# A Hedgehog attention with an S4 convolution on one core: second products of ten far rows as extra moving columns, near tables for two quarters, output weights last

## The chip, the core and the metric

The kernel runs on one core of a Trainium2 chip. The metric is the device time of the launch in microseconds (us). The profile is one execution recorded by the hardware profiler; its engines are PE (TensorE: PE for the matmuls, PEld for the weight loads that overlap them), DVE (VectorE), ACT (ScalarE), POOL (GpSimd) and SP (SyncE, which issues nearly all DMAs here).

## The reference

Two independent branches whose outputs stand side by side in one array of 2048 x 896 in bf16. The first is linear attention with learned softmax features, 16 heads of 28 features:

```python
qkv = x @ wqkv                                   # x: 1 x 2048 x 448
pq = einsum("bhsd,hdf->bhsf", q, w_phi); pk = einsum("bhsd,hdf->bhsf", k, w_phi)
phi_q = concat([softmax(pq), softmax(-pq)]); phi_k = concat([softmax(pk), softmax(-pk)])
kv = einsum("bhsf,bhsd->bhfd", phi_k, v); z = phi_k.sum(over s)
o = einsum(phi_q, kv) / (einsum(phi_q, z) + 1e-6)
a = o @ wo
```

The second is a state-space convolution over 448 channels with 256 complex states each:

```python
l = arange(2048).astype(bf16)                    # rounded: 641 different positions are left
P = exp(dt * A * l);  K = einsum("dn,dnl,dn->dl", C, P, dt * B).real
y = irfft(rfft(pad(u)) * rfft(pad(K)), 4096)[:2048]   # length 4096, per channel
b = y + u * Dskip
```

## The kernel before

**How the order is set.** The kernel does not issue instructions as its Python functions run. Each helper appends a pair (engine, function) to a list, 1008 of them, and `prog.run(ORDER)` at the end issues them in the order of a written-out list of numbers. Three more lists belong to it: `PLACES` gives the SBUF address of each buffer, `SLOTS` the PSUM banks of each group of matmuls, and `PICKS` says for each of 200 copies and scalings whether ScalarE (A) or VectorE (V) does it. Every engine works through its own part of the order in sequence. Since the helpers issue everything, the profile's lines are theirs: L177 `tt` (VectorE, two tensors), L194 `recip` (VectorE reciprocal), L198 `af` (ScalarE, any function), L205 `copy`, L208 `scaled`, L211 `square`, L215 `mset` (POOL), L220 `mms` (matmuls), L230 `transposes`, L236 and L240 the DMAs. So one reads the profile by shape.

**The convolution.** The 448 channels are worked in four quarters (`qt`) of 112; a quarter has QC = 224 columns (a state half for each channel) on 128 partitions, and NCOL = 896 columns are all four. A position is written as one of 16 high parts plus one of 40 low parts (`HI`, `LO`), so that exp(dt A l) is a product. For one quarter, `tables` makes

- the near low rows: `args` lets TensorE multiply the angles and dampings (AT, TH, each held as a bf16 part and a bf16 rest) by scaled identities of PID into PSUM, `rotations` takes sine and cosine, `dampings` exp of plus and minus multiples, and `damp` multiplies these into rows 2 to 15 of W;
- the far low rows: `far` makes rows 16 to 39. `step` adds 256 to the positions of some rows by a complex product with PW[256], which is two products, one subtraction and one addition on VectorE; `squares` doubles the positions of four rows;
- the high rows U_, in `hi_tables`, by doubling;
- the kernel K at all positions: `build_k` contracts the states on TensorE. One accumulation runs on 32 of the array's columns, so four groups (g) work side by side, and 80 columns move (40 low rows by two channels). A copy moves the sums to TS, and `scatter_k` sends them through DRAM to the layout that the transform reads (KT).

`kernel_spectrum` transforms KT (matmuls of 112 columns against the table F), `signal_spectrum` does the same to u, in two halves, after adding and subtracting u and its reversal; the reversed odd rows are made by TensorE with a reversal matrix (REV), and the result waits in DRAM (SUd). `conv` multiplies the spectra on VectorE (`prod`), combines the products either on VectorE (`finish`) or, for the blocks in `ON_PE`, on TensorE (`finish_pe`), and transforms back in `inverse`, 36 matmuls of 112 columns for each block, of which four add u times Dskip.

**The attention.** `fold_weights` multiplies the query and key weights by w_phi. `key_side` runs over eight pairs of row tiles: matmuls for K and V, exponentials of both signs, a transposing DMA (ET), the softmax sums on TensorE, their reciprocals on VectorE, and the state sums kv, which gather in PSUM over all eight pairs (matmuls of 116 columns, L220, whose moving operand VR holds 4 of every 16 values). At the end it multiplies the states by the output weights once, M = KV @ wo, with eight transposes and eight matmuls. `query_side` takes four blocks of 512 rows: query matmuls, exponentials, denominators and reciprocals, a trip through DRAM (SCd) that spreads the softmax weights over partitions (SB), the product EQ = EQ x SB, and 32 matmuls of 448 columns with M.

**The order around the change.** The program calls, in this order, `tables(0)`, `key_side`, `tables(1)`, then query blocks, spectra, convolutions and the other two `tables`; `ORDER` interleaves them far more finely. On SP's queue stand the loads of parameters, of u (four loads of 0.46 MB), of the table G1, of weights and the transposing loads of x.

## Time and profile before

| what | value |
|---|---|
| device time, three runs | 235.61, 237.11 and 239.20 us; median 237.11 us |
| span of the profiled execution | 233.5 us (the record gives no separate time of that execution; the median is 3.6 us above its span) |
| busy PE / DVE / ACT | 208.1 / 216.8 / 183.9 us |
| instructions | 7103, of them 3044 on PE |
| DMA | 36.40 MB, 156 GB/s on average |
| chain that ended last | PE 51%, ACT 17%, DVE 13%, DMA 5% of the span |

A busy time sums the durations of an engine's instructions. Matmuls are pipelined, so a matmul's duration holds latency that overlaps the next one; the distance from one start to the next is the better price. In a row such as "L220 PE MATMUL psum<-sbuf 128\*32 128x80 bf16 x896 | 18.3, 258 | 0.0" stand the line, the engine, the operation, where it writes and reads, the shape (for matmuls the stationary tile and the moving operand), the count, the busy time of all, the mean duration of one in ns, and the idle time before them. A row of a stretch gives from and to, and then the busy times of PE, PEld, DVE, ACT and POOL with the instructions in brackets, the clock granted to TensorE (1.00 is full), the busy share of the DMA engines and what they moved in GB/s. A row of the chain gives the start, the length, the engine and the line.

### The profile page before, as it was taken

The numbers are of one execution on the slowest core, as the hardware profiler recorded it, in microseconds if no ns is written. First come the engines' busy times: TensorE is split into PE (matmuls) and PEld (weight loads), VectorE is DVE, ScalarE is ACT, GpSimd is POOL, SyncE is SP. The second block draws the span as 40 slices with busy tenths as digits, with TensorE's granted clock in tenths as the row PEclk, the third lists the DMA queues.
The fourth block names the chain that finished last, engine by engine and source line by source line (L and its number), as shares of the span: only waits on it lengthen the run. The fifth ranks groups of instructions, "written<-read, shape, count | busy, mean of one in ns | idle before, by whom it ended". The sixth has DMA issues, their size and how long they took to land.

```text
span 233.5 us, 7103 instructions
## 1 busy us (share of the span) xinstructions
PE 208.1 (89%) x3044; PEld 152.8 (65%) x3044; DVE 216.8 (93%) x267; ACT 183.9 (79%) x321; POOL 4.6 (2%) x20
## 2 busy tenths in 40 slices
PE   1173899998999999999987999999999999999994
PEld 1161446564557655589765678885579968689993
DVE  1799999999999999989999979999999999999980
ACT  3999999999999999999998998698328451355331
POOL 4000000000000100000000000000000000000000
PEclk9999999999999999999999999999999999999999
DMA  5999910499239999826865899872696890489643
GB/s 154 237 218 272 151 37 1 167 150 235 71 59 190 147 176 257 152 71 155 206 156 144 99 255 225 226 114 61 70 368 131 199 277 10 63 185 242 121 100 81
DMA packets 81640, 36.40 MB, mean 156 GB/s; under 512 B 65480, under 2 KB 79688, under 8 KB 81224
## 3 DMA queue, kind: packets, MB, share of 16 engines
q1 hardware_dynamic: 81368, 35.71, 73.3%
q8 instruction: 24, 0.39, 0.7%
q10 hardware_dynamic: 240, 0.23, 0.3%
q14 instruction: 8, 0.07, 0.1%
HBM read 19.44 MB, written 8.62 MB: 120 GB/s over the span
## 4 chain that ended last, share of the span: by engine, by line
PE 51%; ACT 17%; DVE 13%; DMA 5%; issue 3%; SPq 0%; ACTq 0%
PE psum L220 51%; DVE sbuf L177 11%; ACT sbuf L198 8%; ACT sbuf L205 7%; DMA sbuf<-sbuf 3%; DMA sbuf<-KTd 2%; ACT L198 1%; DVE sbuf L205 1%; DVE sbuf L194 0%; ACT sbuf L211 0%; SPq L240 0%; DVE sbuf L212 0%; ACT sbuf L208 0%; DVE sbuf L208 0%; PE psum L230 0%
## 5 line engine op out<-in xcount | busy, mean ns | idle before, releaser
L220 PE MATMUL psum<-sbuf 128*128 128x112 bf16 (+9 forms) x3000 | 206.2, 252 | 21.4 <-ACT sbuf L205 7.8
L177 DVE TENSOR_TENSOR sbuf<-sbuf 128x896 bf16<-128x896 bf16 (+11 forms) x222 | 197.3, 956 | 7.2 <-ACT sbuf L198 4.3
L220 PEld LDWEIGHTS <-sbuf 128*128 128x128 bf16 (+3 forms) x3000 | 150.1, 114 | 75.3 <-issue 18.2
L205 ACT CAST sbuf<-psum 128x448 bf16<-128x448 f32 (+4 forms) x129 | 79.7, 672 | 38.0 <-PE psum L220 37.3
L198 ACT ACTIVATE sbuf<-psum 128x448 bf16<-128x448 f32 (+4 forms) x110 | 65.5, 721 | 0.5 <-PE psum L220 0.4
L211 ACT ACTIVATE sbuf<-sbuf 128x896 bf16<-128x896 bf16 x14 | 14.2, 1024 | 4.0 <-DVE sbuf L177 4.0
L198 ACT ACTIVATE sbuf<-psum,sbuf 128x896 f32<-128x896 f32 (+3 forms) x17 | 13.6, 835 | 0.0
L208 ACT ACTIVATE sbuf<-sbuf 128x896 bf16<-128x896 bf16 (+2 forms) x10 | 10.9, 1091 | 1.4 <-DVE sbuf L299 0.8
L198 ACT ACT_TABLE_LOAD x8 | 10.3, 1283 | 1.4 <-PEq L900 1.3
L205 ACT COPY sbuf<-sbuf 128x224 bf16<-128x224 bf16 (+2 forms) x18 | 8.9, 512 | 0.0
L205 DVE CAST sbuf<-psum 128x448 bf16<-128x448 f32 (+3 forms) x8 | 5.3, 690 | 2.3 <-PE psum L220 1.7
L215 POOL MEMSET sbuf<- 128x224 bf16 (+4 forms) x15 | 4.2, 314 | 153.3 <-PE psum L220 153.1
L205 ACT COPY sbuf<-psum 112x896 bf16<-112x896 bf16 (+2 forms) x13 | 6.8, 549 | 0.1
L177 DVE TENSOR_TENSOR sbuf<-psum,sbuf 128x448 bf16<-128x448 f32 (+3 forms) x12 | 5.1, 444 | 0.1
L194 DVE RECIPROCAL sbuf<-psum 128x64 bf16<-128x64 f32 x8 | 4.3, 546 | 0.4 <-ACT sbuf L198 0.3
L230 PEld LDWEIGHTS <-sbuf 112*112 112x112 bf16 (+1 forms) x44 | 3.1, 128 | 1.8 <-DVE sbuf L177 0.8
L230 PE MATMUL psum<-sbuf 112*112 112x112 bf16 (+1 forms) x44 | 3.6, 215 | 0.6 <-DVE sbuf L177 0.6
L212 DVE TENSOR_TENSOR sbuf<-sbuf 128x896 bf16<-128x896 bf16 (+1 forms) x3 | 3.3, 1087 | 0.0
L194 DVE RECIPROCAL sbuf<-sbuf 128x64 f32<-128x64 f32 x4 | 2.2, 545 | 0.0
L189 DVE SCALAR_TENSOR_TENSOR sbuf<-sbuf 128x64 f32<-128x64 f32 (+1 forms) x5 | 2.0, 393 | 0.0
L205 ACT CAST sbuf<-sbuf 128x1792 bf16<-128x1792 f32 x1 | 1.8, 1814 | 0.0
L208 DVE TENSOR_SCALAR sbuf<-sbuf 128x1568 bf16<-128x1568 bf16 (+1 forms) x3 | 1.6, 538 | 0.0
(8 smaller groups left out, 2.1 us busy)
## 6 DMA issues: line engine op xcount, KB each, us to landing
SUd<-sbuf SPq DMA_DIRECT2D x8, 448.0 KB
sbuf<-SCd SPq DMA_DIRECT2D x16, 224.0 KB
sbuf<-SUd SPq DMA_DIRECT2D x4, 896.0 KB
sbuf<-const SPq DMA_DIRECT2D x3, 1024.0 KB
sbuf<-const SPq DMA_DIRECT2D x8, 384.0 KB
sbuf<-in_B_u_dram SPq DMA_DIRECT2D x4, 448.0 KB
out_dram<-sbuf SPq DMA_DIRECT2D x4, 448.0 KB
out_dram<-sbuf SPq DMA_DIRECT2D x16, 112.0 KB
```

The lines of the kernel that those rows point to most:

```text
L177: prog.add("V", lambda: nc.vector.tensor_tensor(out=o, in0=a, in1=b, op=op))
L189: prog.add("V", lambda: nc.vector.scalar_tensor_tensor(out=o, in0=a, scalar=s, in1=b, op0=op0, op1=op1))
L194: nc.vector.reciprocal(o, a)
L198: prog.add("A", lambda: nc.scalar.activation(o, a, fn, **kw))
L205: either(lambda: nc.scalar.copy(o, a), lambda: nc.vector.tensor_copy(o, a))
L208: either(lambda: nc.scalar.activation(o, a, ACT.Copy, scale=s), lambda: nc.vector.tensor_scalar_mul(o, a, s))
L211: either(lambda: nc.scalar.activation(o, a, ACT.Square), lambda: nc.vector.tensor_tensor(out=o, in0=a, in1=a, op=ALU.mult))
L212: lambda: nc.vector.tensor_tensor(out=o, in0=a, in1=a, op=ALU.mult))
L215: prog.add("G", lambda: nc.gpsimd.memset(o, v))
L220: nc.tensor.matmul(o, lhsT=l, rhs=r, **kw)
L230: nc.tensor.transpose(o, i, idn)
```

## The change

- **Far rows.** W gets 52 rows (`N_W`) instead of 40. `step` now stores only the first of its two products. For ten rows the second product goes to rows 40 to 51 of W instead of into a temporary; `build_k` moves all 52 rows (104 columns), and one VectorE addition of 336 elements adds the extra rows' sums to those of rows 20 to 23, 28 to 31 and 36 to 39 in TS (two of the extra rows are cleared by POOL after use). For five rows the second product is still added on VectorE (`plus`). The squares are always made by ScalarE with a factor of the square root of a half, so that rows come halved and no doubling is needed; the table F carries the missing factors (`GROWN`). The order of the low rows is new.
- **Near tables.** `rotations` and `dampings` make the tables of two quarters at once, in steps of 448 columns, reading AT and TH (now f32) from SBUF; `args` and its matmuls are gone, and PID has two matrices instead of six. The negation of the dampings moves into `dampings`.
- **Signal.** A DRAM to DRAM copy (`turn_u`) turns the odd rows of u, eight loads take the place of four, and TensorE reverses nothing. The transform reads its moving operand in a permuted order; the spectra of the kernel are copied without the permutation that they had, and `inverse` reads its moving operand in the order 0, 7, 1, 8, ... of each 14 columns.
- **Reciprocals.** All are made on ScalarE as Ln and then Exp with scale -1; a table set that holds both is asked for when a stretch of them begins.
- **Output weights last.** M is gone. For each query block NT = KVN^T EQ is made by eight matmuls of 512 columns and four copies, and 16 matmuls of 448 columns with wo follow.
- **Others.** The last doubling of `hi_tables` uses a negated power (N128), two products of halves and one addition. The exponentials of queries come two banks at a time. `ON_PE` gains (2, 1). Loads of WV and Wqk change places.
- **Lists.** `ORDER` (1022 steps), `PLACES`, `SLOTS` and `PICKS` (189 picks) are new throughout. In the new order the turning copy stands seventh on SP's queue, ahead of the loads of u, G1 and the weights.

```diff
...
+N_W = 52
 QC = 224
 NCOL = 4 * QC
-ODD = [1, 3, 5, 7]
-LO = [0, 8] + [s * p for p in (2, 4, 6, 1, 3, 5, 7) for s in (-1, 1)]
-LO += [256 + p for p in LO[0:8]]
-LO += [2 * LO[i] for i in (16, 18, 19, 21)]
+MULT = (6, 4, 2, 3, 1, 5, 7)
+LO = [0, 8] + [s * p for p in MULT for s in (-1, 1)]
+LO += [256 + LO[i] for i in (0, 7, 6, 5, 4, 3, 2, 1)]
...
 LO += [256 + p for p in LO[24:28]]
-LO += [2 * LO[i] for i in (24, 26, 28, 30)]
+LO += [2 * LO[i] for i in (24, 25, 28, 29)]
...
-ON_PE = [(0, 1), (1, 1)]
-SPLIT = [[(0, QC)]] * 4
+GROWN = [1, 1, 1, 2, 8]
+ON_PE = [(0, 1), (1, 1), (2, 1)]
...
+            F[blk, kt, r] += GROWN[kt] * np.stack([even.real, odd.real, even.imag, odd.imag])
...
-    def recip(o, a):
-        def fn():
-            with nc.allow_low_precision(reason="bf16 softmax weights, as in the reference"):
-                nc.vector.reciprocal(o, a)
-        prog.add("V", fn)
+    def recip(o, a, ln):
+        af(ln, a, ACT.Ln)
+        af(o, ln, ACT.Exp, scale=-1.0)
 
     def af(o, a, fn, **kw):
-        prog.add("A", lambda: nc.scalar.activation(o, a, fn, **kw))
+        def do():
+            kind = {ACT.Sin: "sin", ACT.Exp: "exp", ACT.Ln: "exp"}.get(fn)
+            if kind == "exp" and prog.kind != "exp":
+                nc.scalar.preload_act_table_set("natural_log_exp_and_others")
+            prog.kind = kind or prog.kind
+            nc.scalar.activation(o, a, fn, **kw)
+        prog.add("A", do)
...
-    def row_pairs(row, a):
+        cols = slice(512 * i, 512 * i + 512)
+        for j in range(3):
+            dma_t(xT[:, j, cols], x2, 512 * i, 1, 512, 128 * j)
+        dma_t(xT[:, 3, cols], x2, 512 * i, 1, 512, 320)
+
+    ue = [sb([128, 4, D_MODEL]) for _ in range(2)]
+    uo = [sb([128, 4, D_MODEL]) for _ in range(2)]
+
+    def turn_u():
         rs = u2.ap[0][0]
-        return bass.AP(tensor=u2.tensor, offset=u2[row + 128 * (1 - a), 0].offset,
-                       ap=[[2 * rs, 64], [256 * rs, 4], [1, 2 * D_MODEL]])
-
-    ua = [sb([128, 4, 2, D_MODEL]) for _ in range(2)]
+        dma("S", URd.rearrange("(g i) d -> g i d", g=16),
+            bass.AP(tensor=u2.tensor, offset=u2[127, 0].offset, ap=[[128 * rs, 16], [-2 * rs, 64], [1, D_MODEL]]))
 
     def load_u(b):
+        rs = u2.ap[0][0]
         for a in range(2):
-            dma("S", ua[b][64 * a:64 * a + 64].rearrange("p t r d -> p t (r d)"), row_pairs(1024 * b, a))
+            p = slice(64 * a, 64 * a + 64)
+            dma("S", ue[b][p], bass.AP(tensor=u2.tensor, offset=u2[1024 * b + 128 * (1 - a), 0].offset,
+                                       ap=[[2 * rs, 64], [256 * rs, 4], [1, D_MODEL]]))
+            src = URd[64 * (8 * b + 6 + a), 0:1]
+            dma("S", uo[b][p], bass.AP(tensor=src.tensor, offset=src.offset,
+                                       ap=[[D_MODEL, 64], [-128 * D_MODEL, 4], [1, D_MODEL]]))
...
+    turn_u()
     load_u(0)
     load_u(1)
...
-    AT = sb([128, 2, NCOL])
-    TH = sb([128, 2, NCOL])
+    AT = sb([128, NCOL], F32)
+    TH = sb([128, NCOL], F32)
...
-        ab = sb([128, 2, 4, D_MODEL])
-        ur = sb([128, 4, D_MODEL])
-        for tp in range(2):
-            bs = prog.banks(2)
-            mms([(psum[:, bs[k], 0:D_MODEL], REV, ua[b][:, 3 - 2 * tp - k, 1, :], dict(start=True, stop=True))
-                 for k in range(2)])
-            copy(ur[:, 2 * tp:2 * tp + 2, :], two(bs))
-        add(ab[:, 0], ua[b][:, :, 0, :], ur)
-        sub(ab[:, 1], ua[b][:, :, 0, :], ur)
+        ab = (ue[b], sb([128, 4, D_MODEL]))
+        sub(ab[1], ue[b], uo[b])
+        add(ue[b], ue[b], uo[b])
...
-                                     [(G1[:, cp, jt, 128 * mt:128 * mt + 128], ab[:, cp ^ st, jt, :])
+                                     [(G1[:, cp, jt, 128 * mt:128 * mt + 128], view(ab[cp ^ st][:, jt, 0:1], [14, 32], [1, 2], [2, 7]))
...
-    def args(src, qt):
-        cols = slice(qt * QC, (qt + 1) * QC)
-        items = []
-        bs = prog.banks(2)
-        for e in range(4):
-            at = (e % 2) * QC
-            items += acc(psum[:, bs[e // 2], at:at + QC], [(PID[:, e, :], src[:, part, cols]) for part in range(2)])
-        mms(items)
-        return psum[:, bs[0], 0:1], 512 * (bs[1] - bs[0])
...
     def rotations(qt):
...
+        T = sb([128, 2, 7, 2 * QC])
+        for c_ in range(2):
+            for r, m in enumerate(MULT):
+                af(T[:, c_, r, :], TH[:, qt * QC:qt * QC + 2 * QC], ACT.Sin, scale=float(m), **(dict(bias=bias_hp) if c_ == 0 else {}))
         return T
...
     def dampings(qt):
...
+        A = sb([128, 21, 2 * QC])
+        for i in range(2):
+            for r, m in enumerate(MULT):
+                af(A[:, 3 * r + i, :], AT[:, qt * QC:qt * QC + 2 * QC], ACT.Exp, scale=float((2 * i - 1) * m))
+        scaled(A[:, 2:21:3, :], A[:, 1:20:3, :], -1.0)
         return A
...
-        def step(s0, d0, n):
-            t = sb([128, 2, n, w])
-            mul(t, at(0, s0, n), pw(1, n))
-            mul(at(0, d0, n), at(0, s0, n), pw(0, n))
-            sub(rows_(0, d0, n), rows_(0, d0, n), t[:, 1])
-            add(rows_(1, d0, n), rows_(1, d0, n), t[:, 0])
...
+    def far(W, qt):
+        X = W[:, :, N_LO:N_W, :]
+
+        def times_far(o, s0, d, n):
+            mul(o, view(W[:, 1, s0, 0:1], [-WS, 2], [d * QC, n], [1, QC]),
+                view(P256[:, 0, qt * QC:qt * QC + 1], [NCOL, 2], [0, n], [1, QC]))
+
+        def step(s0, d, d0, n):
+            mul(view(W[:, 0, d0, 0:1], [WS, 2], [1, n * QC]), view(W[:, 0, s0, 0:1], [WS, 2], [d * QC, n], [1, QC]),
+                view(P256[:, 2, qt * QC:qt * QC + 1], [0, 2], [0, n], [1, QC]))
+
+        def plus(d0, n, t):
+            o = W[:, :, d0:d0 + n, :]
+            add(o, o, t)
...
-                square(sq[i].rearrange("p (a b) x -> p a b x", a=2), four(i, s0, ka, kb))
+                af(sq[i].rearrange("p (a b) x -> p a b x", a=2), four(i, s0, ka, kb), ACT.Square, scale=HALF)
             mul(four(1, d0, 2, 1), four(0, s0, ka, kb), four(1, s0, ka, kb))
-            scaled(rows_(1, d0, 4), rows_(1, d0, 4), 2.0)
-            sub(rows_(0, d0, 4), sq[0], sq[1])
-        copy(view(W[:, 0, 16, x0:x0 + 1], [WS, 2], [1, w]),
-             PW[256][:, :, qt * QC + x0:qt * QC + x0 + w])
-        step(1, 17, 7)
-        squares(16, 3, 2, 24)
-        step(24, 28, 4)
-        squares(24, 4, 2, 32)
-        step(32, 36, 4)
-
+            sub(W[:, 0, d0:d0 + 4, :], sq[0], sq[1])
...
+        step(7, -1, 17, 7)
+        t = sb([128, 2, 3, QC])
+        times_far(t, 7, -1, 3)
+        plus(17, 3, t)
+        times_far(X[:, :, 0:4, :], 4, -1, 4)
+        squares(16, 2, 1, 24)
+        step(24, 1, 28, 4)
+        times_far(X[:, :, 4:8, :], 24, 1, 4)
+        plus(28, 2, X[:, :, 4:6, :])
+        mset(X[:, :, 4:6, :], 0.0)
+        squares(24, 4, 1, 32)
+        step(32, 1, 36, 4)
+        times_far(X[:, :, 8:12, :], 32, 1, 4)
...
-                                      view(W[:, ri, 0, x:x + 1], [QC, N_LO], [1, 2]),
+                                      view(W[:, ri, 0, x:x + 1], [QC, N_W], [1, 2]),
...
-            recip(VR[:, :, :, D_HEAD, :], psum[:, bz, 0:64].rearrange("p (t s h) -> p t s h", t=2, s=2))
+            LN = sb([128, 4, 16], F32)
+            recip(view(VR[:, 0, 0, D_HEAD, 0:1], [(D_HEAD + 1) * 16, 4], [1, 16]),
+                  psum[:, bz, 0:64].rearrange("p (a h) -> p a h", a=4), LN)
...
-        p = bank16(*prog.banks(1), [112, 8, 112])
-        transposes([(p[:, i, :], KVN[:, i // 4, i % 4].rearrange("p h d -> p (h d)"), id112) for i in range(8)])
-        copy(KVT, p)
-        for ip in range(4):
-            b = prog.banks(2)
-            mms([(psum[0:112, b[k], 0:D_MODEL], KVT[:, 2 * ip + k, :], wo[:, (2 * ip + k) % 4, :],
-                  dict(start=True, stop=True)) for k in range(2)])
-            copy(M[:, 2 * ip:2 * ip + 2, :], two(b, 112))
...
+        EQ8 = EQ.rearrange("p s c t -> p (s c) t")
+        mul(EQ8, EQ8, SB)
+        NT = sb([112, 4, 512])
+        for c in range(4):
+            (b,) = prog.banks(1)
+            mms(acc(psum[0:112, b, :], [(KVN[:, s, c].rearrange("p h d -> p (h d)"), EQ[:, s, c, :]) for s in range(2)]))
+            copy(NT[:, c, :], psum[0:112, b, :])
         of = sb([128, 4, D_MODEL])
         for t4 in range(4):
             (b,) = prog.banks(1)
-            mms(acc(psum[:, b, 0:D_MODEL], [(EQ[:, i // 4, i % 4, 128 * t4:128 * t4 + 128], M[:, i, :])
-                                            for i in range(8)]))
+            mms(acc(psum[:, b, 0:D_MODEL], [(NT[:, c, 128 * t4:128 * t4 + 128], wo[:, c, :]) for c in range(4)]))
...
-                copy(view(sk[:, b, 0, m // 4, m % 4, 0:1], [896, 2], [14, 16], [2, 7], [1, 2]),
-                     view(psum[:, bk, 0:1], [224, 2], [14, 16], [1, 7], [7, 2]))
+                copy(view(sk[:, b, 0, m // 4, m % 4, 0:1], [896, 2], [1, 224]), view(psum[:, bk, 0:1], [224, 2], [1, 224]))
...
-                                 [(GI[:, r, cp, mt, 128 * jt:128 * jt + 128], S[:, r, cp, 112 * mt:112 * mt + 112])
+                                 [(GI[:, r, cp, mt, 128 * jt:128 * jt + 128], view(S[:, r, cp, 112 * mt:112 * mt + 1], [14, 8], [1, 7], [7, 2]))
...
-        T = rotations(qt)
+        if qt % 2 == 0:
+            near[:] = rotations(qt), dampings(qt)
...
-            far(W, qt, x0, w)
-            for c in range(x0 // 112, (x0 + w) // 112):
-                build_k(W, U_, TS, c)
+        damp(W, near[1], near[0], qt)
+        far(W, qt)
+        for c in range(2):
+            build_k(W, U_, TS, c)
+        add(*(2 * [view(TS[:, 20, 0:1], [8 * 28, 3], [1, 4 * 28])]), TS[:, N_LO:N_W, :].rearrange("p (a l) x -> p a (l x)", a=3))
         scatter_k(qt, TS, KT[qt])
...
```

More of the change, by code (lines that the diff above doesn't have):

```diff
@@ L334 @@
         for nch in range(2):
-            o0, o1 = (view(dst[:, part, 56 * nch:56 * nch + 1], [112, 8], [1, 2], [2, 28]) for part in range(2))
-            i = view(psum[:, b[nch], 0:1], [56, 8], [28, 2], [1, 28])
-            copy(o0, i)
-            sub(o1, i, o0)
+            copy(view(dst[:, 56 * nch:56 * nch + 1], [112, 8], [1, 2], [2, 28]),
+                 view(psum[:, b[nch], 0:1], [56, 8], [28, 2], [1, 28]))
     prods = {}
@@ L449 @@
     mset(one128, 1.0)
[L451 to L476 removed]
+    WS = N_W * QC
@@ L599, in key_side @@
                 (b4,), (b5,) = prog.banks(1), prog.banks(1)
[L600 to L601 removed]
+                for bk, w_ in ((b4, Wp[1]), (b5, WV)):
+                    mms(acc(psum[:, bk, 0:D_MODEL], [(xT[:, dj, ts_], w_[:, dj, :]) for dj in range(4)]))
                 for s in range(2):
```

144 lines of the change are left out of this document (55 added, 89 removed), and 103 rows, old and new, of tables (ORDER, PLACES, SLOTS).

## The prediction

> **What bounds the kernel now.** I read the page's busy times first, then busy time by stretch, then the chain of waits, and last the groups by shape. Part 1 of the page:
>
> ```profile
> span 233.5 us, 7103 instructions
> ...
> PE 208.1 (89%) x3044; PEld 152.8 (65%) x3044; DVE 216.8 (93%) x267; ACT 183.9 (79%) x321; POOL 4.6 (2%) x20
> ```
>
> VectorE is the busiest over the whole span, which would make it the engine to relieve. The same numbers by stretch, and the end of the chain, say otherwise. The stretches (columns: PE, weight loads, DVE, ACT, POOL, each with its instructions, granted clock, DMA share, GB/s):
>
> ```profile
> 0.00:30.00 30.00, 14.02 (x90) 9.64 (x91) 23.29 (x26) 26.12 (x36) 2.51 (x12) 1.00 0.95 204
> 30.00:129.69 99.69, 93.71 (x1215) 61.87 (x1213) 98.09 (x136) 98.37 (x176) 1.58 (x6) 1.00 0.67 139
> 129.69:230.10 100.41, 100.37 (x1742) 81.31 (x1741) 95.39 (x107) 58.90 (x111) 0.51 (x2) 1.00 0.77 162
> ```
>
> The chain of waits from 129 us on (start, length, what):
>
> ```profile
> 129.69 31.20 PE psum L220 x553
> 160.89 0.06 PE psum L230
> 160.94 12.11 PE psum L220 x64
> 173.05 0.06 PE psum L230
> 173.11 56.97 PE psum L220 x1087
> 230.07 0.02 issue
> 230.10 0.53 ACT sbuf L205
> ```
>
> So there are two stages. Up to 129.69 us ScalarE and VectorE are full (98.4 and 98.1 of 99.7 us) and TensorE, though it looks busy, has waits: its 1215 matmuls there are fewer than the 1742 of the equally long stretch behind. From 129.69 to 230.07 us TensorE never waits, ScalarE is idle two fifths of the time, and the chain is matmuls alone. The end is therefore (moment at which TensorE stops waiting) + (matmul work left at that moment) + 3.4 us for the last copy and store (233.5 - 230.1). VectorE saved in the second stage is worth nothing, unless it makes TensorE wait.
>
> **Prices.** A matmul is priced from start to start, because its duration in the groups holds latency. TensorE by stretch (busy, instructions):
>
> ```profile
> 103.86:108.94 5.08, 5.08 (x101) 1.00 0.44 93
> 192.97:197.37 4.40, 4.40 (x226) 1.00 0.06 8
> 207.96:211.50 3.54, 3.54 (x77) 1.00 1.06 293
> 211.50:213.97 2.47, 2.47 (x52) 1.00 0.95 311
> ```
>
> Each count holds a few that were started before. In order these are six blocks of 16 state-sum matmuls of 116 columns (96 in 5.08 us: 52.9 ns), the 14 blocks of one `build_k` (224 in 4.40 us: 19.6 ns for 80 columns on a quarter of the array), four first-half blocks of `kernel_spectrum` (72 in 3.54 us: 49.2 ns for 112 columns), four second-half blocks (48 in 2.47 us: 51.5 ns). The 64 matmuls of 448 columns in the chain row of 12.11 us give 189 ns; 512 columns then take 216. Check on the old second stage, counted from the order list: 128 x 189 + 64 x 189 + 576 x 49.2 + 252 x 49.2 + 192 x 51.5 + 448 x 19.6 + 8 x 216, and some 3 us of small ones, is 100.0 us; measured 100.4.
>
> ScalarE's steps, likewise from start to start:
>
> ```profile
> 5.89 4.15 ACT L198 ACTIVATE sbuf<-psum 128x896 f32<-128x896 f32 x5 [0.38 <-PE psum L220]
> 61.84 1.91 ACT L198 ACTIVATE sbuf<-psum 128x448 bf16<-128x448 f32 x4
> L198 ACT ACTIVATE sbuf<-psum 128x448 bf16<-128x448 f32 x44 | 23.6, 663 | 0.0
> L205 ACT COPY sbuf<-sbuf 128x448 bf16<-128x448 bf16 x8 | 5.0, 623 | 0.0
> L198 ACT ACTIVATE sbuf<-psum 128x224 bf16<-128x224 f32 x12 | 4.8, 411 | 0.1
> L211 ACT ACTIVATE sbuf<-sbuf 128x896 bf16<-128x896 bf16 x14 | 14.2, 1024 | 4.0 <-DVE sbuf L177 4.0
> L198 ACT ACTIVATE sbuf<-psum 128x896 f32<-128x896 f32 x10 | 8.9, 959 | 0.4 <-PE psum L220 0.4
> L198 ACT ACTIVATE sbuf<-psum,sbuf 128x896 f32<-128x896 f32 x5 | 5.2, 1077 | 0.0
> ```
>
> Four steps of 896 elements take (4.15 - 0.96) = 3.2 us, 0.80 each; three of 448 take (1.91 - 0.66), 0.42 each; so 512 elements take 0.48, 224 some 0.25, and the squares of 896 from SBUF 0.85.
>
> **The change, stage one: when does TensorE stop waiting?** In the new list the last time TensorE must wait for ScalarE is the first output block of query block 1: it needs all four new NT copies of that block. I count the ScalarE instructions in the list up to the fourth of them, against those that the old trace had done by 129.69 us. More: 13 query exponentials that were later before (6.2 us), 4 NT copies (1.9), 3 spectrum copies (1.3), 22 steps of Ln and Exp on 64 elements that replace VectorE's reciprocals (some 0.14 each, 3.1), 4 squares (3.4), one f32 square of 1792 (1.6). The near tables: all four quarters now lie ahead of this point as 56 steps of 448 from SBUF, against 42 steps before (14 each of 896, 448 and 224: 11.2 + 5.9 + 3.5 = 20.6). No row reads f32 from SBUF in this shape. The nearest, the SBUF copy of 448, lasts 623 ns against 663 for an exponential from PSUM, so not longer: 0.42 is the lower end; the rows with a bias column (1,077 ns where 896 without it take 959) add 0.1 for half of them: upper end 0.55. I take 0.47, so 26.3, which is 5.7 more (2.9 to 10). Less: 3 copies of the reversed signal, 4 of M and one of its transpose (8 x 0.8 = 6.4), 3 doublings of squares (2.6), and a dozen copies and scalings that the new picks give to VectorE (together 8.8, net of a few small ones that come to ScalarE). Sum: 23.2 - 17.8, some 5.4 us later, so 135 us. The removed matmuls of this stage (16 `args` blocks, the reversal, M) are worth nothing: TensorE was waiting there. So are the strided reads that the signal's transform now makes.
>
> Two edits could add a wait here. The copy that turns the odd rows of u in DRAM stands seventh on SP's queue; the four loads of turned rows wait for it to land, and behind them queue the DFT table, the Q/K weights and all transposes of x. Up to the turned rows of the first half the queue then moves 3.2 MB (six raw arrays of 0.23 MB, the turning of 0.92 MB, two halves of 0.46), at 204 GB/s some 16 us, and the half sums on VectorE can start near 18 us; in the list they stand behind the negated dampings, which ScalarE delivers near 15. ScalarE, the bound, has ten sines to do meanwhile, so I cost this at 0 (0 to 3 us if the cover is short). The POOL clearing of two rows waits for VectorE and has a square and a product to hide behind: 0.
>
> VectorE itself loses about 13 us:
>
> ```profile
> L177 DVE TENSOR_TENSOR sbuf<-sbuf 128x1792 bf16<-128x1792 bf16 x44 | 46.1, 1081 | 0.0
> L177 DVE TENSOR_TENSOR sbuf<-sbuf 128x3136 bf16<-128x3136 bf16 x16 | 28.2, 1783 | 0.4 <-ACT sbuf L205 0.4
> L177 DVE TENSOR_TENSOR sbuf<-sbuf 128x1568 bf16<-128x1568 bf16 x8 | 7.5, 957 | 0.0
> L177 DVE TENSOR_TENSOR sbuf<-sbuf 128x896 bf16<-128x896 bf16 x74 | 43.0, 617 | 2.3 <-ACT sbuf L211 1.8
> L194 DVE RECIPROCAL sbuf<-psum 128x64 bf16<-128x64 f32 x8 | 4.3, 546 | 0.4 <-ACT sbuf L198 0.3
> ```
>
> The far rows of a quarter took 2 x 1.78 + 2 x 0.96 + 4 x 1.08 + 4 x 0.62 = 12.3 us and take 1.78 + 5 x 1.08 + two of 1,344 (0.85) + 0.62 = 9.5: 11 us over four quarters. The 12 reciprocals save 6.5, one `finish` on TensorE 4.5, four subtractions from PSUM go (2.2), and some 11 come back with the copies. It ended at 226.8 us, 3 us ahead of TensorE:
>
> ```profile
> 210.60 16.20 DVE L177 TENSOR_TENSOR sbuf<-sbuf 128x896 bf16<-128x896 bf16 x18
> ```
>
> A VectorE that ends earlier leaves the end to TensorE.
>
> **Stage two: the matmul work left.** From the list, after that first output block: 64 of 448 columns for outputs (12.1), 24 of 512 for NT (5.2), 96 of 448 for three quarters finished on TensorE instead of two (18.1), 360 of `kernel_spectrum`, now all contiguous (17.7), 448 of `build_k` (8.8), 576 of `inverse` (28.3): 90.2 us, where the old stage had 100.4. The 14 more copies that ScalarE makes there (12 of NT, 2 of the third finish) fall into its idle time.  Two prices are added, and both lie bare on the path.
>
> The first: `build_k` moves 104 columns instead of 80.
>
> ```profile
> L220 PE MATMUL psum<-sbuf 128*32 128x80 bf16 x896 | 18.3, 258 | 0.0
> L220 PE MATMUL psum<-sbuf 128*128 128x112 bf16 x1064 | 55.4, 213 | 4.0 <-ACT sbuf L205 2.6 <-DMA sbuf<-KTd 1.5
> ```
>
> 80 columns in pairs 448 bytes apart last longer (258 ns) than 112 side by side (213), so the reading seems to set the pace, and 30% more of it costs up to 30%: 2.6 us here. The lower end is 0, if issuing four quarters takes the 78 ns anyhow. I take 2.6. The Trainium skill (TensorEngine Tiling, Key Properties) says that tiles of the array load and multiply independently; by that 104 columns fit under the others and the sum is 2.6 lower; no run here shows it.
>
> The second: `inverse` now reads its moving operand with the order 0, 7, 1, 8, 2, 9, ... in 512 of 576 matmuls. The trace has two strided readers. State sums read 4 of every 16 columns: 52.9 ns for 116, against 51 by the price of 112 side by side. In the second-half spectrum blocks 4 of 12 matmuls read every second element: 51.5 against 49.2, so 3 x 2.3 = 7 ns for each strided one. I take the 7: 3.5 us, with 0 as the lower end; the upper end is a rival below.
>
> Sum: 135 + 90.2 + 2.6 + 3.5 = 231.3; + 3.4 is a span of 234.7 against 233.5. The median of the runs (237.1) lies 3.6 over the span of the profiled execution, so the time is 238.3; I say 239 us for small waits of the new list. What was late is late again: TensorE starts its unbroken stretch 5 us later with 10 us less to do, and gets 6 of them back as slower reads.
>
> **Rivals.** A: strided reading is dear, so slower. The order of `inverse` jumps 14 bytes ahead and 12 back at each column, which neither reader of the trace does; both take at least two columns from most places before they move on. If each column becomes a read of its own at half pace, a matmul takes 98 ns and 512 of them 25 us in place of 3.5: 260 us. At three times the pace it would be 285, and if only the extra 7 ns double or triple, 245. For it speak the 7 ns, and the 258 ns of 80 columns in pairs; against it the state sums, whose jumps cost almost nothing. From some 14 ns a matmul on the time is over 2% longer. The Trainium skill (SBUF — State Buffer, Door 1: The DMA port swizzle) says that SBUF is read in lines of 16 bytes, with two hits a line needed for full pace. By that rule most reads of `inverse` are single hits and A's time follows; the 7 ns, where most lines have more than two hits, are more than the rule gives.
>
> B: faster. Patterns cost nothing (-3.5), the 104 columns hide (-2.6), and SBUF sources are as quick as PSUM ones (0.42: -2.8): 229.5 us. For it speak the state sums and the SBUF copy; against it the 7 ns, and that the three must come together.
>
> C: the change does not do what it says: the table set with both Ln and Exp is asked for once in a stretch, but if a table load is set between each Ln and Exp all the same, a dozen pairs cost two loads each.
>
> ```profile
> L198 ACT ACT_TABLE_LOAD x8 | 10.3, 1283 | 1.4 <-PEq L900 1.3
> ```
>
> 24 x 1.28 is 31 us, nearly all ahead of 135 us: near 267.
>
> **How the numbers follow.** I give the forecast 0.40, A 0.28, B 0.29, C 0.03. The measurement tells some 2% from no change. The forecast is within 2% in 0.30, slower in 0.08 (strided reads a little dearer, 3 us of late rows), faster in 0.02; A and C are slower; B is faster in 0.25 and within 2% in 0.04. Together: faster 0.27, same 0.34, slower 0.39. The range reaches from B's time, less a little, to the half-pace case: 228 to 262; the forecast's own is 233 to 245.
>
> **What would show it.** TensorE's unbroken chain begins near 135 us and has about 96 us of matmuls. An `inverse` block (36 matmuls) goes from 1.77 to 2.0 us if the 7 ns hold, to 3.4 in A, and stays in B. A `build_k` of one quarter goes from 4.4 to 5.7 us. VectorE ends some us ahead of the last matmul, and table loads number seven. The forecast is wrong if the chain begins ahead of 130 us, if VectorE or a landing stands in the chain behind 140 us, or if a block of `inverse` leaves 1.8 to 2.1 us.

## The result and the profile after

The changed kernel takes 264.51 us (median of 4 runs, 262.77 to 266.9), the kernel before 236.36 us (median of 4): 1.12 times as long, 95% interval 1.104 to 1.136. The forecast was 239 us, its range 228 to 262. The profiled execution spans 261.1 us, 27.6 us more than before.

Part 1 of the page of the changed kernel:

```profile
span 261.1 us, 6954 instructions
PE 229.0 (88%) x2956; PEld 169.2 (65%) x2956; DVE 206.6 (79%) x249; ACT 178.8 (68%) x342; POOL 8.4 (3%) x24
```

VectorE and ScalarE work less than before (206.6 against 216.8 us, 178.8 against 183.9); TensorE works 21 us more, on 88 instructions fewer. The chain of waits of the changed kernel (start, length, what):

```profile
28.74 25.09 PE psum L227 x104
...
129.91 4.62 DMA sbuf<-SCd
134.73 3.05 DVE sbuf L180 x2
137.92 1.55 DVE sbuf L180 x5
140.33 2.71 DMA sbuf<-KTd
143.14 5.93 PE psum L227 x56
149.12 108.41 PE psum L227 x1440
```

TensorE's last long wait ends at 143.14 us, where the first output block starts, not at 135. The chain puts this wait down to a load of KT, but the block reads NT and the output weights wo, and no KT. In the run e1 below, the row of the same block names the load of wo (first line), and SP issues that load late: in the changed kernel at 135.61 us (second line), in the kernel before at 111.71.

```profile
143.28 4.16 PE L227 MATMUL psum<-sbuf 112*128 112x448 bf16 x20 [0.47 <-DMA sbuf<-in_A_wo_dram]
135.61 0.32 SPq L247 DMA_DIRECT2D sbuf<-in_A_wo_dram  x1
```

By the semaphore events of the trace wo has landed at 143.00 us and the block starts at 143.14; in the runs e1, e2, e8 and e9 it starts as close behind this landing (0.13 to 0.14 us), while the loads of KT are still landing. The last of the four NT copies that the block needs had ended at 142.16, so the late weights cost it about 1 us.

There is also a stretch of 25 us, early, in which the signal's transform on TensorE alone holds the path. Busy time by stretch in the changed kernel, each stretch within one kind of work (columns: PE, weight loads, DVE, ACT, POOL, clock, DMA share, GB/s):

```profile
35.97:46.58 10.61, 10.61 (x50) 4.59 (x48) 10.27 (x14) 10.44 (x17) 0.74 (x1) 1.00 0.36 93
203.15:208.77 5.62, 5.62 (x227) 5.39 (x225) 4.63 (x4) 2.48 (x5) 0.00 (x0) 1.00 0.01 3
242.10:254.30 12.20, 12.20 (x147) 12.20 (x145) 2.33 (x5) 3.34 (x7) 0.00 (x0) 1.00 0.45 88
```

The first is six blocks of the signal's transform, 48 matmuls of 448 columns: 221 ns each, where 448 columns took 189. The second is one `build_k`: 224 matmuls in 5.62 us, 25.1 ns, against 19.6. The third is four blocks of `inverse`, 144 matmuls: 84.7 ns each, against 49.2. A block takes 3.05 us instead of 1.77, and there are 16 blocks on TensorE's unbroken stretch: 20.5 us.

To see the rest, both kernels are cut at the same point of the computation, the start of `build_k` of quarter 1 (all keys done). Before, and then the changed kernel:

```profile
30.00:111.40 81.40, 78.29 (x908) 50.38 (x905) 79.81 (x102) 81.07 (x144) 1.07 (x4) 1.00 0.67 135
111.40:230.10 118.70, 115.79 (x2054) 92.80 (x2052) 113.68 (x141) 76.19 (x143) 1.03 (x4) 1.00 0.76 161
```

```profile
30.00:115.60 85.60, 79.59 (x840) 47.53 (x837) 78.78 (x97) 80.81 (x154) 4.25 (x9) 0.98 0.60 132
115.60:257.60 142.00, 138.02 (x2052) 114.74 (x2052) 108.96 (x134) 73.92 (x155) 2.71 (x6) 1.00 0.59 136
```

The changed kernel reaches this point 4.2 us later and needs 23.3 us longer from there. TensorE is busy 97% of that time in both kernels, so it sets it in both, and its work grew by 22.2 us.

### The profile page after: what moved, and what is told of

Same layout as the page of the kernel before. It is cut to its first block, busy times and chain, and to the rows that moved or that the text cites. A ratio compares the mean times of both kernels' runs of the same rounds, so it can differ in the third digit from the quotient of the medians.

```text
span 261.1 us, 6954 instructions
## 1 busy us (share of the span) xinstructions
PE 229.0 (88%) x2956; PEld 169.2 (65%) x2956; DVE 206.6 (79%) x249; ACT 178.8 (68%) x342; POOL 8.4 (3%) x24
## 4 chain that ended last, share of the span: by engine, by line
PE 62%; ACT 17%; DVE 11%; DMA 4%; issue 4%; SPq 1%; ACTq 0%; DVEq 0%
PE psum L227 62%; ACT sbuf L204 12%; DVE sbuf L180 9%; ACT sbuf L212 5%; DMA sbuf<-SCd 2%; DVE sbuf L212 2%; DMA sbuf<-in_B_log_dt_dram 1%; DMA sbuf<-KTd 1%; SPq L247 1%; ACT L204 0%; DVE sbuf L192 0%; PE psum L237 0%; ACTq L204 0%; DVEq L180 0%; ACTq L212 0%
## 5 line engine op out<-in xcount | busy, mean ns | idle before, releaser
L227 PE MATMUL psum<-sbuf 128*128 128x112 bf16 (+9 forms) x2920 | 227.3, 265 | 27.9 <-DVE sbuf L180 12.0
L227 PEld LDWEIGHTS <-sbuf 128*128 128x128 bf16 (+4 forms) x2920 | 167.2, 114 | 87.1 <-issue 25.7
L180 DVE TENSOR_TENSOR sbuf<-sbuf 128x1792 bf16<-128x1792 bf16 (+12 forms) x205 | 185.9, 968 | 15.0 <-ACT sbuf L204 6.3
L212 ACT CAST sbuf<-psum 128x448 bf16<-128x448 f32 (+4 forms) x129 | 76.4, 639 | 71.9 <-PE psum L227 68.7
L204 ACT ACTIVATE sbuf<-sbuf 128x448 bf16<-128x448 f32 (+4 forms) x89 | 49.8, 616 | 1.9 <-DMA sbuf<-in_B_log_dt_dram 1.4
L204 ACT ACTIVATE sbuf<-psum 128x448 bf16<-128x448 f32 (+3 forms) x82 | 44.1, 677 | 3.1 <-DVE sbuf L212 3.0
L212 DVE CAST sbuf<-psum 128x448 bf16<-128x448 f32 (+3 forms) x14 | 10.6, 782 | 17.6 <-PE psum L227 12.0
L222 POOL MEMSET sbuf<- 128x224 bf16 (+5 forms) x19 | 8.0, 442 | 180.5 <-DVE sbuf L180 60.6
L204 ACT ACTIVATE sbuf<-psum,sbuf 128x896 f32<-128x896 f32 x5 | 5.0, 1021 | 0.7 <-DVE sbuf L212 0.7
L212 ACT COPY sbuf<-psum 128x128 f32<-128x128 f32 (+2 forms) x11 | 5.1, 475 | 0.1
```

The source lines that it names most:

```text
L180: prog.add("V", lambda: nc.vector.tensor_tensor(out=o, in0=a, in1=b, op=op))
L204: nc.scalar.activation(o, a, fn, **kw)
L212: either(lambda: nc.scalar.copy(o, a), lambda: nc.vector.tensor_copy(o, a))
L222: prog.add("G", lambda: nc.gpsimd.memset(o, v))
L227: nc.tensor.matmul(o, lhsT=l, rhs=r, **kw)
```

## Experiments

The theory after the result: the order in which TensorE reads its moving operand is what costs, in `inverse` above all. The rivals: something else about the new kernel slows these blocks (addresses, transfers beside them), or the loss lies in the first stretch, with ScalarE.

**Reading side by side again.** e1 moves the permutation to the copy out of PSUM and builds DD permuted:

```diff
-    view(S[:, r, cp, 112 * mt:112 * mt + 1], [14, 8], [1, 7], [7, 2])
+    S[:, r, cp, 112 * mt:112 * mt + 112]
-    copy(OB.rearrange("p t x -> p (t x)"), psum[:, bk, 0:D_MODEL])
+    copy(view(OB[:, 0, 0:1], [14, 32], [2, 7], [1, 2]), view(psum[:, bk, 0:1], [14, 32], [1, 7], [7, 2]))
```

> The changed kernel, but inverse reads its moving operand side by side again; the permutation of each 14 channels is made in the copy that takes the result out of PSUM, and the skip's diagonal (DD) is built in the permuted order. In the changed kernel a block of 36 matmuls takes 3.05 us, in the kernel before 1.77. Theory (the order of reading alone costs this): blocks return to about 1.77 us, 16 x 1.28 = 20.5 us go, and all of it lies on the unbroken chain, so about 244 us. Rival (the blocks are slow for another reason, such as the buffers' new addresses or transfers beside them): blocks stay above 2.5 us and the time above 258 us.

Measured: 246.04 us, 1.040 times before (1.032 to 1.048). 18.5 us of the 28 are gone. Five blocks near its end, 180 matmuls and the few that were started before:

```profile
228.13:236.98 8.85, 8.85 (x184) 8.85 (x182) 6.83 (x8) 4.31 (x9) 0.00 (x0) 1.00 0.66 124
```

That is 1.77 us a block. The rival falls.

e2 does the same for the signal, in the copies `sg`:

```diff
-    view(ab[cp ^ st][:, jt, 0:1], [14, 32], [1, 2], [2, 7])
+    ab[cp ^ st][:, jt, :]
-    copy(sg[...], two(bs)...)
+    for each of the two banks: copy(view(sg[:, 0, 2 * mp + k2, 0:1], [448, 4], [14, 8], [1, 14]),
+                                    view(psum[:, bs[k2], 0:1], [14, 32], [1, 2], [2, 7]))
```

> As the run before, and the signal's transform too reads side by side; its permutation is made in the copies from PSUM, one bank at a time. In the changed kernel its 128 matmuls of 448 columns start 221 ns apart, before 189. Theory (the reading cost 128 x 32 ns = 4.1 us where TensorE alone held the path, from 28.7 to 54 us): about 240 us, with the unbroken chain starting some 4 us earlier than at 149 us. Rival (ScalarE is the bound of the first stage, and TensorE's slow transform only took up slack): under 1.5 us of difference to the run before.

Measured: 243.22 us, 1.028 (1.020 to 1.035). By the medians the signal's reading cost 2.8 us; the two intervals overlap, but the trace agrees: the first output block starts at 140.66 us instead of 143.28 in e1. All further runs on the changed kernel start from e2.

e3 puts the order 0, 7, 1, 8 into the kernel before and changes nothing else:

> The kernel before with one edit: inverse reads in the order 0, 7, 1, 8, ... of each 14 columns (the convolution's channels then come out in another order). Theory: 512 matmuls of the 576 gain 36 to 40 ns each, all on TensorE's unbroken stretch: 19 to 21 us, so about 256 us, and no other change in the trace. Rival (the price belongs to the changed kernel's surroundings): under 8 us.

Measured: 257.47 us, 1.091 (1.080 to 1.101), 20.9 us more. The price does not depend on the rest of the change.

**The price of a reading order.** e4 runs TensorE alone.

> TensorE alone: none of the reference's computation, only rows of 48 matmuls of 112 moving columns on a 128 x 128 stationary tile, one row for each order of reading, and four rows of 96 matmuls on 32 columns of the array. Theory A (a read returns 16 bytes and only neighbours in the same 16 bytes share it): the order 0, 7, 1, 8 and every 8th element cost the same, near twice the 49 ns of side by side; 0, 2, 1, 3 costs nothing extra. Theory B (any step that is not +1 costs, whatever its size): 0, 2, 1, 3 costs as much as 0, 7, 1, 8. Theory C (jumps back cost): every 2nd, 4th, 8th element are free and 0, 8, 1, 9 is dear. Four groups on pairs 224 elements apart: 19.6 ns a matmul for 80 columns and about 24 for 104, as in the kernels; if reading sets that, side by side is quicker, if issuing does, it is the same.

The chain of its trace has a row for each order (one line of the code each; these are the ones used below):

```profile
28.53 2.36 PE psm L50 x48
33.29 4.28 PE psm L52 x48
37.57 5.12 PE psm L53 x48
42.69 2.36 PE psm L54 x48
45.05 5.12 PE psm L55 x48
52.52 2.72 PE psm L57 x48
55.24 2.40 PE psm L58 x48
57.65 4.86 PE psm L59 x48
62.51 9.60 PE psm L60 x48
72.11 9.76 PE psm L61 x48
81.87 4.96 PE psm L62 x48
86.83 4.64 PE psm L63 x48
91.47 2.44 PE psm L64 x48
```

| order of 112 columns (line) | ns a matmul |
|---|---|
| side by side (L50), 0 2 1 3 (L54) | 49 |
| every 2nd element (L58); fours, 16 elements apart (L64) | 50, 51 |
| 0 2 4 .. 12, 1 3 .. 13, as the signal's transform reads (L57) | 57 |
| 0 7 1 8, as `inverse` reads (L52) | 89 |
| 0 8 1 9 (L53), 0 64 1 65 (L55) | 107 |
| every 4th (L59); pairs, 16 or 224 apart (L62, L63) | 101; 103, 97 |
| every 8th (L60), every 16th (L61) | 200, 203 |

Eight strided matmuls of 89 and one of 49 make the 84.7 of `inverse`. Theory B falls with L54 and theory C with L59. Theory A's picture, reads of 16 bytes, fits steps in one direction, but not with the price that it gave: with four or more bf16 values from the same 16 bytes the pace is full, with two it halves, with one it is a quarter (A had every 8th element near half pace). Each new 16 bytes then costs 1.8 ns (200/112 and 101/56), and every 16th element costs no more than every 8th. It is not the whole rule: A had 0 7 1 8 equal to every 8th element, and it costs less than half; 0 8 1 9 and 0 64 1 65 take a new 16 bytes at every column and cost half of what every 8th does. How a return to 16 bytes read just before is served stays open. The Trainium skill (SBUF — State Buffer, Door 1: The DMA port swizzle) asks for two hits a line of 16 bytes; measured, two are not enough for TensorE: pairs take 97 to 103 ns.

The four groups of 32 columns, pairs and then side by side, 80 columns:

```profile
101.07 1.96 PE psm L68 x87
103.03 0.86 PE psm L69 x96
```

Pairs take some 20 ns a matmul, side by side 9: reading pairs, not issuing, sets the pace of `build_k`, so more columns cost in proportion (104 in pairs: 25.1 in the stretch of `build_k` above).

**The 2.8% that are left.** The forecast without its 3.5 us for strided reads would have been 235.5 us; e2 takes 243. Two single parts first:

> Base: the kernel that reads both operands side by side (e2_both_side, 243.2 us). One edit: no copy that turns the odd rows of u; the odd rows are loaded straight from u in their own order, so the spectrum of u is that of wrong sums. TensorE waits there for the value weights until 59.9 us, whose load is issued at 53.4 us behind the long queue. Theory (the queue is late because of the turning copy and the loads that wait for it, and the key side starts late for it): the key matmuls start 3 to 5 us earlier and the time falls by 2 to 4 us. Rival (the transposing loads of x hold the queue, the turning hides): under 1 us.

> Base: e2_both_side. One edit: build_k moves 40 rows again instead of 52 and the addition of the extra rows is left out, so the ten far rows lack their second product. Theory (reading pairs sets the pace, and 104 columns cost 24.2 ns a matmul where 80 cost 19.3): 448 matmuls behind the start of the last stretch save 2.2 us, the other 448 up to 2.2 where TensorE held the path, so 2 to 4 us. Rival (the extra columns hide under ScalarE and VectorE): under 1 us.

e5, without the turning copy: 241.72 us, 1.020 (1.012 to 1.029); the keys start at 59.5 us instead of 59.9. The copy costs 1 to 2 us at most. e6, with 40 rows moved: 242.27 us, 1.022 (1.015 to 1.029), about 1 us less. Both intervals overlap that of e2, and neither part alone is the cause.

Then work was taken from the engines.

> Base: e2_both_side. One edit: the 14 exponentials of the dampings of quarters 0 and 1, which ScalarE makes from 9.7 us on, ahead of every sine, are left out; POOL fills their rows with ones. ScalarE loses 14 x 0.47 = 6.5 us at its start. Theory (ScalarE sets the first stretch, as the forecast had it): 6 to 7 us faster. Rival (the first stretch is set further on, by VectorE and by landings): the sines, and the signal's matmuls that wait for their banks, come 6 us earlier, but the end gains under 3 us.

> Base: e2_both_side. One edit: the 28 sines and exponentials of the near tables of quarters 2 and 3 are left out, and POOL fills their rows. All lie ahead of the first output block, so ScalarE loses 28 x 0.47 = 13 us there, and two table loads. Theory (ScalarE sets the first stretch): about 13 us faster, or as far as the next engine lets it, 8 us at least. Rival (VectorE and TensorE are nearly as full): under 4 us.

```diff
-    af(A[:, 3 * r + i, :], AT[...], ACT.Exp, ...)
+    if qt == 2: mset(A[:, 3 * r + i, :], 1.0)      # e8: qt == 0; e9: the sines of T likewise
+    else: af(A[:, 3 * r + i, :], AT[...], ACT.Exp, ...)
```

e8: 240.97 us, 1.012 (1.004 to 1.020), 2 to 4 us less, nearer its rival (under 3) than its theory (6 to 7). e9: 243.70 us, 1.022 (1.016 to 1.029): 13 us less for ScalarE gain about 1 at most, by the medians nothing. In e9 the fourth NT copy of the first output block ends at 138.37 us, 2.0 earlier than in e2, but wo has landed only at 140.29, and TensorE waits:

```profile
140.43 2.03 PE L227 MATMUL psum<-sbuf 112*128 112x448 bf16 x5 [2.90 <-DMA sbuf<-KTd]
```

So ScalarE's work at the very start counts in part, and its 13 us behind that hardly do: most of them turn into waits of its own, and what is left the load of wo takes back. Whether an earlier load of wo would let more of it through was not tried.

> Base: e2_both_side. One edit: the 12 VectorE products that fill the extra rows of W (three of 1792 elements for each quarter, 1.08 us each) are left out; POOL fills the rows with zeros, so the ten far rows lack their second product. VectorE loses 13 us over the whole span, as much as ScalarE lost in e9_no_tables23, which gained 1 us. Theory (VectorE sets what is left of the loss, in both stretches): 6 to 13 us faster than e2. Rival (no engine sets it; the waits of one engine for another, in the order of the lists, do): under 3 us, as with ScalarE.

> Base: e2_both_side. As e13_less_vector, but for quarters 0 and 1 alone, whose far rows lie ahead of the first output block: VectorE loses 6.5 us in the first stretch. Theory (VectorE sets the first stretch): 4 to 6.5 us faster than e2. Rival (the first stretch is set by waits between engines, the second by VectorE): under 2 us.

e13: 242.46 us, 1.019 (1.009 to 1.029); e14: 242.31 us, 1.021 (1.006 to 1.035). 13 us less for VectorE gain 1 to 2 us. POOL's fills, 18.8 us of work in e13, stand nowhere in its chain. And e2 has this from the common point on:

```profile
113.50:236.00 122.50, 117.87 (x2052) 94.28 (x2052) 110.10 (x134) 74.29 (x155) 2.71 (x6) 1.00 0.68 154
```

TensorE is nearly as full as in the other two, with 117.87 us of work against 115.79 before. That suggested to take from TensorE:

> Base: e2_both_side. One edit: the second block of quarter 2 is finished on VectorE again (one addition of 3584 elements, a subtraction and an addition of 896, two of 896 for the halves, at the places of TensorE's work), as in the kernel before, instead of by 32 matmuls of 448 columns and two copies. TensorE loses 6.05 us, VectorE gains 4.5. Theory (from the start of build_k of quarter 1 TensorE sets the time: it is busy 117.9 of the 122.5 us left there, and the runs that took 13 us from ScalarE or from VectorE gained little): 3 to 6 us faster than e2, so within 1.5% of the kernel before. Rival (waits in the order of the lists set it): under 2 us.

> As e15_vector_21, and the second block of quarter 1 too goes back to VectorE: TensorE loses 12.1 us, VectorE gains 9, which brings it to some 119 us of work in the 122 that are left at build_k of quarter 1. Theory (TensorE sets the time until VectorE does): no faster than e15 by more than 2 us, perhaps slower by up to 3. Rival (waits): within 2 us of e2.

e15: 245.55 us, 1.042 (1.035 to 1.050); e16: 249.23 us, 1.053 (1.044 to 1.062). Both are slower. Less for TensorE does not help when VectorE must do it: in e2 VectorE stands in the chain between 164 and 196 us, ahead of the blocks of quarter 2.

```profile
163.94 3.40 DVE sbuf L180 x3
167.34 1.36 issue
168.69 9.97 DVE sbuf L180 x8
178.69 0.86 DVE sbuf L180
179.81 1.01 DVE sbuf L180
181.50 2.71 DVE sbuf L180 x4
184.23 2.10 DVE sbuf L180 x2
```

**Reciprocals, and the order at the start.**

> Base: e2_both_side. One edit: the 12 reciprocals are made by VectorE in one step each, as in the kernel before, instead of Ln and Exp on ScalarE. ScalarE loses 24 steps of some 0.14 us from start to start (3.4 us), VectorE gains 12 of 0.55 (6.6 us). Theory (ScalarE is the bound up to the last stretch): 1 to 3 us faster. Rival (VectorE, which in this base stands in the chain from 164 to 196 us and from 100 to 113, is as much of a bound): no gain, or up to 3 us slower.

> Base: e2_both_side. One edit: the 12 reciprocals are made by VectorE at the place of the Ln, with a copy of 64 elements on VectorE at the place of the Exp (the run e7_vector_recip made them at the place of the Exp alone, after the bank that they read had been given to other sums). ScalarE loses 24 steps, 3.4 us; VectorE gains 12 x (0.55 + 0.2) = 9 us. Theory (ScalarE sets the first stretch): 1 to 3 us faster. Rival (VectorE is as much of a bound): 2 to 5 us slower.

> Base: the kernel before. One edit taken from the change: its 12 reciprocals as Ln and Exp on ScalarE at the same places, with the table set that holds both. VectorE loses 6.5 us, ScalarE gains 24 steps of 0.14 us, 3.4. Theory (VectorE is the bound of the first stretch in the kernel before too, as the runs on the changed kernel say of that): 2 to 4 us faster than the kernel before. Rival (ScalarE, 98.4 of 99.7 us busy there, is the bound, as the forecast had it): 0 to 4 us slower.

> Base: e2_both_side. All of its work, in another order at the start: the load of A_im ahead of the other parameters on SP's queue and its matmuls right behind those of A_re, ScalarE's ten sines of the powers ahead of the 14 exponentials of the dampings (which follow the near sines), and with them VectorE's first two products of the far chain; two sines of quarter 2 go behind the key exponentials. Theory (the new list lets VectorE and TensorE wait at the start, since the sines hold the banks of the signal's transform until 28.7 us): the signal's matmuls start 4 to 6 us earlier and the time falls by 2 to 4 us, as far as e8_no_damp01 fell without those steps. Rival (e8 gained by the steps that it left out, not by their place): under 1 us, or slower, since the far chain of quarter 0 starts later.

e7 (246.81 us) made them where their bank held other sums already, so it measured another wait than meant; e10 stands in its place: 248.81 us, 1.046 (1.037 to 1.055), 4 to 6 us slower than e2. On the changed kernel Ln and Exp on ScalarE are the better choice, as far as e10 tells, which also adds a small copy for each. On the kernel before they are the worse one: e12 takes 246.03 us, 1.039 (1.032 to 1.046), some 9 us more, twice what its rival allowed, with two more table loads (eight before, ten here):

```profile
L196 ACT ACT_TABLE_LOAD x5 | 6.4, 1283 | 1.3 <-PEq L909 1.2
L198 ACT ACT_TABLE_LOAD x5 | 6.4, 1283 | 0.1
```

In e12 the Exp stands right behind its Ln, and a pair takes some 0.4 us from its first start to the next step, not 0.28. Twelve pairs and the two loads are some 7.5 us more for ScalarE, which was full in the first stretch of this kernel, as the forecast read it; the rest stays open. e11, the sines first: 250.63 us, 1.055 (1.048 to 1.063), 6 to 7 us slower than e2. The rival had named this side, but not the size. The run does not show that the place of the steps is worth nothing: it put the dampings behind the near sines, and what needs them waits longer.

No run beats the kernel before.

## Why the prediction was wrong

The forecast span was 234.7 us, the measured one 261.1: of the 26.4 us between them 17.0 are the reads of `inverse` (20.5 instead of 3.5), 8.1 the moment at which TensorE stops waiting, and 1.3 the rest of the matmul work and the last store.

**The price of strided reads in `inverse`: the term that failed.** The forecast took 7 ns a matmul, from the second-half blocks of `kernel_spectrum`, 3.5 us in all. It is 40 ns for each strided one (89 against 49), 20.5 us in all. The step that failed was the choice of the row: these blocks read every second element, where four values still come from each 16 bytes, and the order 0, 7, 1, 8 leaves them at most columns. Rival A had the mechanism and nearly the price, 98 ns and 260 us; e1, e3 and e4 show the mechanism. That its time comes so near is partly luck: its 25 us for these reads are 4.5 too many, and its 135 us for the start are 8 too few. It was given 0.28, and most of the 0.39 that the prediction gave to a slower kernel came from it; the sum itself forecast about no change. The row that spoke for it, 80 columns in pairs at 258 ns, was in the prediction, and e4 confirms what it said: reading pairs sets the pace of `build_k`.

**The strided reads of the signal's transform, put at nothing because TensorE was said to wait there: wrong.** 128 matmuls at 221 instead of 189 ns are 4.1 us, and the chain shows TensorE alone from 28.74 to 53.83 us. e2 returns 2.8 us.

**The moment at which TensorE stops waiting, 135 us: it was 143.14.** The forecast counted ScalarE's steps up to the fourth NT copy of the first output block. Their prices held: the new table steps, for instance, start 0.466 us apart (0.47 was taken):

```profile
9.71 6.16 ACT L204 ACTIVATE sbuf<-sbuf 128x448 bf16<-128x448 f32 x13
```

So did their sum. Up to 129.69 us ScalarE had been busy for 26.12 + 98.37 = 124.5 us in the kernel before; with the forecast's 5.4 more that is 129.9. In the changed kernel it is busy for 23.60 + 107.15 = 130.8 us up to 142.16, the end of the fourth copy:

```profile
0.00:30.00 30.00, 11.44 (x68) 6.91 (x69) 18.88 (x21) 23.60 (x35) 1.46 (x9) 0.94 0.88 213
30.00:142.16 112.16, 103.23 (x1321) 66.59 (x1318) 102.91 (x143) 107.15 (x217) 4.75 (x11) 0.98 0.64 143
```

What failed is that ScalarE would be as full up to there as before, and that nothing but its copies holds the block. It waited 11.4 us instead of 5.2, which is 6.2 of the 8.1 us (4.1 of the waits behind 30 us are for TensorE's sums); 0.9 are more work, and 1.0 is the load of wo, which the forecast did not count. In the chain a landing of SCd and VectorE stand ahead of that load's issue, and e9 shows that 13 us of ScalarE's work are worth about 1 at most. The prediction had named a landing behind 140 us as a sign against itself.

**The matmul work left in stage two.** The count was right but for `inverse`: 12.1 + 5.2 + 18.1 + 17.7 + 11.2 + 48.8 is 113.1 us, and from 143.14 to 257.55 TensorE took 114.4. The comparison with the old stage was not: it set 90 us from one point against 100 from another. From the same point on, TensorE has as much to do as before even with both reading orders undone (117.9 against 115.8 us), because, by the counts, NT, the third finished block and the 104 columns replace what M and the shorter outputs saved. Between the common point and the cut TensorE was busy for 15.4 us before and for 23.6 in the changed kernel: 1.2 of these 8.2 us are the wider `build_k`, and 7 of the 10 us of relief were work that now lies ahead of the cut.

**`build_k` with 104 columns, 2.6 us:** the price was right. A quarter takes 5.6 us (5.7 was forecast). From e2, where the stretch is broken by other waits, e6 returns about 1 us, less than its own theory of 2 to 4.

**VectorE and the table loads:** right. VectorE lost 10 us (13 forecast), and the changed kernel ends with matmuls alone from 149 us on; table loads number seven:

```profile
L202 ACT ACT_TABLE_LOAD x4 | 5.1, 1283 | 1.3 <-PEq L889 1.2
L204 ACT ACT_TABLE_LOAD x3 | 3.8, 1283 | 0.0
```

**The turning copy, cost at 0 with 0 to 3 us as its bounds:** inside them; e5, on the base of e2, puts it at 1 to 2 us.

**What stays open.** Of the 7.0 us between the spans of e2 (240.5) and of before (233.5), 2.1 lie ahead of the common point, 2.1 are more TensorE work behind it, 1.7 are more waits there and 1.1 a later last store. Taking 13 us from ScalarE (e9) or VectorE (e13) returns about 2 us at most, 6.5 us at ScalarE's start (e8) 2 to 4; giving VectorE 4.5 to 9 more costs 2 to 6, and the other order at the start about 7. This fits an order in which three engines are nearly full at once, but it is not shown. Whether another order of the same work, with wo loaded earlier for one, would return these 7 us was not tried beyond e11.

## What to carry to other kernels

Before a permutation is moved into a matmul's moving operand, count how many values each 16 bytes gives to neighbouring columns: in e4 four bf16 values read at full pace, two at half, and an order that leaves them at each column and comes back costs about as much as two. The copy out of PSUM took the permutation of `inverse` at no price that e1 shows: ScalarE's copies of 448 columns take 566 ns on average in the changed kernel, 564 in e1. When a wait is put down to a transfer, ask whether the waiting instruction reads what it brings. And compare the work that is left from the same point of the computation: a shorter last stretch may only mean that the cut has moved.

## What the runs showed of the hardware

In e4 TensorE's granted clock fell to 0.50 while it read every 8th and every 16th element, and it came back after that; stretches of the trace (PE busy, granted clock):

```profile
57.60:62.20 4.60, 4.60 (x48) 1.00 0.02 4
66.00:71.60 5.60, 5.60 (x30) 0.50 0.00 0
86.80:91.20 4.40, 4.40 (x49) 1.00 0.00 0
```

The profile counts TensorE as busy throughout, and the grant fell all the same; why is not shown. The step of 8 elements took 200 ns in its first matmuls already, before the clock fell. The pairs 16 apart, some two thirds of them at the lower clock, took 103 ns from first to last, those 224 apart at the full one 97, so in this range reading, not the clock, set the pace. Four groups of 32 columns, side by side, take 36 ns for four matmuls of 80 columns; one alone would take 35 by the 49 ns for 112 (an estimate). This agrees with what the Trainium skill (TensorEngine Tiling (Array Packing), Key Properties) says of independent tiles, that they can multiply in parallel.
